# Pooled attention with a top-1 mixture of experts: other order of the first steps, pooling split anew, bias summed as a ninth head

## The chip, the cores and the metric

One NeuronCore of one Trainium2 chip runs the whole program. The metric is the device time of one execution in microseconds (us); the kernel before has a median of 625.47 us over 3 runs (623.34 to 629.04). Engines are named as in the profile: PE is TensorE (PEld its weight loads), DVE VectorE, ACT ScalarE, POOL GpSimd, and SP issues the DMAs. Each works through its own list of instructions in order.

## The reference, cut to what matters

```
q, k, v: (8 batches, 8 heads, 576 rows, 64)   x: 4608 tokens of 512   8 experts
k_p, v_p = mean of k, v over each 8 rows               # 72 pooled rows per head
attn     = softmax(q k_p^T / 8)                        # per head
x        = attn v_p, heads side by side                # one token per (batch, row)
logits   = x @ w_gate + modality_bias[modality_id]     # 8 per token
e        = argmax(logits);  g = softmax(logits)[e]
out      = g * (relu(x @ w1[e]) @ w2[e])
```

## The kernel before, in words

**Attention** runs in 20 steps. Two batches make five steps: (batch, 0), (batch, 1), a mixed one with the 64 last rows of both batches, then (next batch, 0), (next batch, 1). A step has two tiles of 128 tokens (the mixed one has one), so a group of two batches has 9 tiles. `steps[n]` names batch, half and tiles; the loop at the end of the attention part writes out, for each n, in which order every engine gets its instructions, and puts pieces of later batches in through the lists `hook_0`, `hook_1`, `hook_q`, `hook_2` and `hook_3`. That written order is the schedule: nothing reorders it but PE's early weight loads.

For one batch: `load_k`, `load_v`, `load_q` put DMAs on SP. `pool_k` and `pool_v` sum each 8 rows, either on POOL (`fold`, three additions of halves, L304 to L306) or on DVE (`reduce8`, L309). `k_operand` transposes the pooled keys on PE into `pk` (L340 for chunks 0 to 3 of 128 pooled rows, L343 for the rest) and ACT copies them twice into `kt` (L346, L347). The keys have two parts, chunks 0 to 2 and chunk 3 with the rest. `v_operand` copies the pooled values, multiplied by masks, into `vw` and `v4` (ACT L367, L368; for `v4` DVE or POOL L369) and transposes them (`pv`); `v_gate` multiplies them with the gate's weights (`pg`, L390, L391) into more columns of `vw` and `v4`, so that the product with the probabilities gives each head's share of the logits as well. For `v4` ACT copies the product (L396) and POOL multiplies it by the mask (L397).

For one step and one half w of the heads: `q_pe`, `q_act` transpose the queries (`pq`, L508) and copy them (`qt`, L514); `s_pe` makes the scores (`sc`, L533, mixed L527); `s_dve` takes maximum and difference (`mx` L540, `sb` L543); `s_act` the exponential (`pe`, L555, L556). For one tile: `t_pe`, `t_act` transpose and copy the probabilities (`pp` L562, `pt` L567), `t4_pe`, `t4_act` their last 64 columns (L574, L581); `a_pe` multiplies with the values (`av`, L597, L601); `x_dve` divides (`r`, `lg` L624, `xb` L630) and the rows are stored in DRAM.

**Routing**: when a group's tiles are through, `route` sums the heads' shares (`lgr`, L679), adds the bias (L680), finds maximum, softmax weight, expert and rank. These DVE instructions stand in a list from which `gap()` pops one or two between the instructions of a step. The bias per token, `bias_all`, comes from POOL (`modality_terms`, ending at L457).

**Experts**: 256 tokens to a slot, 18 slots at least (`NSTAT`). `part(s)` runs one slot: for each of 8 pieces f of the hidden width `first` (L170) and `second` (L1160) in three passes each. For the next slot POOL gathers rows (`gather`, L143), scales them (`scale`, L152), and PE transposes them (`x_transposes`, L161); `evac` empties the sums of the slot before, and POOL scatters them to the output (L1142), which `later` can put off until after `scale`.

## Time and profile before

| | |
|---|---|
| runs | 629.04, 623.34, 625.47 us; median 625.47 |
| profiled execution | 627.34 us, span 625.5 us from first to last instruction |
| granted TensorE clock, mean | 0.996 |
| PE busy | 601.5 us (96%) |
| DVE / ACT / POOL busy | 414.8 / 347.6 / 245.8 us |
| DMA | 76.58 MB, mean 122 GB/s |

A row of the timeline has start, time, engine, line, operation and tiles (out<-in), how many instructions it merges, and in brackets how long the engine had been idle and what ended that. A row of the windows has the stretch, its length, busy time and count of each engine in the order PE, PEld, DVE, ACT, POOL, then the granted clock, the DMA engines' busy share and GB/s.

### The profile page before, as it was taken

The page shows a single profiled execution, that of the slowest core. Times are in us where ns is not written, and L with a number is a line of the kernel's source. Part 1 is how long each engine was busy: PE and PEld are TensorE (multiplying, and loading weights), DVE is VectorE, ACT ScalarE, POOL GpSimd, SP SyncE. Part 2 cuts the span into 40 slices and gives each one's busy share as a digit, 9 for nine tenths or more (in the row PEclk, how much of TensorE's full clock was granted, in tenths as well). Part 3 has the DMA queues.
Part 4 walks back from the last instruction along what each step waited for, and adds up shares of the span by engine and source line. Part 5 has one row for each costly group of instructions (what it writes and reads, how often), then busy time and mean ns, then how long its engine had stood idle before and what let it go on. Part 6 is the DMA issues. An engine that isn't in the chain of part 4 may idle for free.

```text
span 625.5 us, 12457 instructions
## 1 busy us (share of the span) xinstructions
PE 601.5 (96%) x4223; PEld 545.5 (87%) x4223; DVE 414.8 (66%) x803; ACT 347.6 (56%) x657; POOL 245.8 (39%) x323
## 2 busy tenths in 40 slices
PE   4899999999999999999999999999999999999996
PEld 3689889888898998999999999999999899999995
DVE  4866798789957578675665665665665665666661
ACT  2667566788541455555555555555555555555551
POOL 5689978663000342422422413522522422422510
PEclk9999899999999999999999999999999999999999
DMA  8999969874202811201201452201205601201200
GB/s 244 287 313 311 357 186 369 279 232 124 86 36 70 271 70 33 69 29 43 70 28 42 130 190 89 67 33 37 70 34 172 202 23 36 69 30 40 70 35 21
DMA packets 63241, 76.58 MB, mean 122 GB/s; under 512 B 15423, under 2 KB 42047, under 8 KB 63168
## 3 DMA queue, kind: packets, MB, share of 16 engines
q1 hardware_dynamic: 57168, 55.98, 28.7%
q0 software_dynamic: 6000, 19.72, 9.7%
q8 instruction: 35, 0.57, 0.4%
q14 instruction: 38, 0.31, 0.2%
HBM read 119.40 MB, written 19.45 MB: 222 GB/s over the span
## 4 chain that ended last, share of the span: by engine, by line
PE 80%; DVE 7%; issue 4%; POOL 3%; DMA 3%; ACT 1%; SPq 0%; POOLq 0%; DVEq 0%; ACTq 0%
PE op L1160 31%; PE hp L170 30%; PE av L597 5%; PE sc L533 3%; PE xt L161 2%; PE av L601 2%; PE pq L508 2%; PE pp L562 2%; PE ph L170 1%; DMA out_dram<-ob,sidx 1%; DMA k<-in_k_dram 1%; DVE sb L543 1%; POOL v L304 1%; DVE mx L540 1%; DVE kp L309 1%
## 5 line engine op out<-in xcount | busy, mean ns | idle before, releaser
L136 ACT CAST hl<-raw 128x1024 fp32r<-128x1024 f32 x138 | 144.8, 1049 | 138.6 <-PE op L1160 137.6
L170 PE MATMUL hp<-xh,hl 128*128 128x256 f32 x1152 | 186.1, 284 | 0.0
L139 DVE TENSOR_TENSOR hl<-raw,hl 128x1024 fp32r<-128x1024 f32 x144 | 179.4, 1247 | 0.0
L170 PEld LDWEIGHTS hp<-xh,hl 128*128 128x128 f32 x1152 | 166.1, 189 | 10.5
L1160 PE MATMUL op<-hl,hh 128*128 128x512 f32 x554 | 173.5, 394 | 0.0
L174 DVE SCALAR_TENSOR_TENSOR hlo<-hp,hh 128x256 fp32r<-128x256 f32 x139 | 58.8, 423 | 132.3 <-ACT hh L172 132.3
L1142 POOL DMA_INDIRECT out_dram<-ob,sidx x36 | 50.4, 1400 | 226.4 <-DVE ob L1136 175.4
L1160 PE MATMUL op<-hl,hlo 128*128 128x512 f32 x277 | 108.4, 391 | 0.0
L1160 PEld LDWEIGHTS op<-hl,hh 128*128 128x128 f32 x554 | 94.8, 189 | 12.1
L170 PE MATMUL hp<-xl,hl 128*128 128x256 f32 x576 | 92.0, 282 | 0.0
L172 ACT ACTIVATE hh<-hp 128x256 fp32r<-128x256 f32 x139 | 53.4, 384 | 49.3 <-PE hp L170 48.9
L170 PEld LDWEIGHTS hp<-xl,hl 128*128 128x128 f32 x576 | 79.0, 190 | 0.0
L143 POOL DMA_INDIRECT xg<-xs,gidx x38 | 41.5, 1092 | 69.3 <-DMA raw<-in_moe_w_dram 53.8
L1160 PEld LDWEIGHTS op<-hl,hlo 128*128 128x128 f32 x277 | 52.0, 188 | 11.8
L152 POOL TENSOR_TENSOR xg<-xg 128x512 f32<-128x512 f32 x34 | 45.0, 1326 | 31.4 <-DMA xg<-xs,gidx 31.3
L597 PE MATMUL av<-vw,pt 128*128 128x146 f32 (+1 forms) x320 | 50.6, 297 | 1.9 <-ACT pt L567 1.1
L597 PEld LDWEIGHTS av<-vw,pt 128*128 128x128 f32 (+1 forms) x320 | 40.5, 183 | 4.1 <-ACT pt L567 2.2
L533 PE MATMUL sc<-kt,qt 128*128 128x144 f32 x256 | 38.5, 295 | 0.0
L533 PEld LDWEIGHTS sc<-kt,qt 128*128 128x128 f32 x256 | 34.8, 198 | 0.2
L540 DVE TENSOR_REDUCE mx<-sc 128x8 f32<-128x576 f32 (+1 forms) x40 | 27.7, 692 | 9.7 <-PE sc L533 8.1
L164 DVE TENSOR_TENSOR xl<-xt,xh 128x512 fp32r<-128x512 f32 x38 | 24.5, 684 | 14.4 <-ACT xh L163 14.4
L601 PE MATMUL av<-vw,pt 128*128 128x146 f32 (+1 forms) x160 | 31.3, 295 | 1.0 <-POOL vw L397 0.8
(234 smaller groups left out, 709.2 us busy)
## 6 DMA issues: line engine op xcount, KB each, us to landing
raw<-in_moe_w_dram SPq DMA_DIRECT2D x304, 256.0 KB
xs<-xb SPq DMA_DIRECT2D x16, 528.0 KB
k<-in_k_dram SPq DMA_DIRECT2D x7, 1024.0 KB
v<-in_v_dram SPq DMA_DIRECT2D x7, 1024.0 KB
q<-in_q_dram SPq DMA_DIRECT2D x6, 1024.0 KB
q<-in_q_dram SPq DMA_DIRECT2D x4, 512.0 KB
v<-in_v_dram SPq DMA_DIRECT2D x16, 128.0 KB
xs<-xb SPq DMA_DIRECT2D x8, 132.0 KB
```

What stands on the lines that cost most here:

```text
L136: nc.scalar.copy(hl[f][:, 0, :], raw[f])
L139: eng.tensor_sub(hl[f][:, 1, :], raw[f], hl[f][:, 0, :].bitcast(F32))
L143: nc.gpsimd.indirect_dma_start(out=xgs[(2 * s + tt) % len(xgs)], out_offset=None, in_=xs[0:rows, :], in_offset=IndirectOffsetOnAxis(idx[:, ...
L152: nc.gpsimd.tensor_tensor(xv, xv, x[:, RX:RX + H].rearrange("p (h o) -> p h o", o=1).to_broadcast([P, H, HD]), op=ALU.mult)
L170: nc.tensor.matmul(ph, hl[f][:, w, d * P:(d + 1) * P], x[:, d, :], start=(n == 0 and d == 0), stop=(n == 2 and d == ND - 1))
L172: nc.scalar.activation(hh, ph, AF.Relu)
L174: nc.vector.scalar_tensor_tensor(hlo, ph, 0.0, hh.bitcast(F32), op0=ALU.max, op1=ALU.subtract)
L533: nc.tensor.matmul(dst, qt[:, i, :], kt[b % NB][:, :, h * SPL:(h + 1) * SPL], start=True, stop=True)
L597: nc.tensor.matmul(av[hs, u, 2 * VC * gg:2 * VC * (gg + 1)], pt[:, c, hs], vw[y][:, c].rearrange("p a x -> p (a x)"), start=(gg == 0), sto ...
L601: nc.tensor.matmul(dst4[hs], pt4[:, hs], v4[y][:, 2 * u:2 * u + 2, :], start=False, stop=True)
L1142: nc.gpsimd.indirect_dma_start(out=out[:, :], out_offset=IndirectOffsetOnAxis(idx.bitcast(U32), 0), in_=ob, in_offset=None, bounds_check=N ...
L1160: nc.tensor.matmul(o[tt], l[:, ts_], hl[f][:, w, D:2 * D], start=(f == 0 and n == 0), stop=(f == NF - 1 and n == 2))
```

## The change

- **Start.** The queries of batch 0 are loaded by heads (4 heads, 1 KB runs) instead of by row pairs (512-byte runs), those of batch 1 in one transfer of 1 KB runs; the last value rows (`v4`) of batch 0 come ahead of the others. The first scores, `s_pe(0, 0)`, stand ahead of the keys' second part. `fill(n)` puts n products of a constant bf16 tile on PE, whose result nobody reads: 20, 5 and 5 after the three first key transposes, 6, 14 and 8 later.
- **Pooling.** Keys of batch 1: chunks 0 and 1 on POOL, 2 and 3 on DVE (before: 0 to 2 on DVE, 3 on POOL). Values of batches 1 and 2: chunk 3 on DVE. Values of batch 0: last rows first.
- **Order.** The keys of batch 1 become operands a little later (first part in `hook_q`, second in `hook_2` of step 1, behind chunk 3's reduction on DVE); the queries of step 3 are transposed in step 2; the values' masks (`v_operand`) stand ahead of the next keys' folds on POOL; `v_gate(0)` stands earlier.
- **Gate.** `v4`'s gate columns are multiplied on DVE straight from PSUM (L415); ACT's copy and POOL's product go.
- **Bias.** POOL copies it into a ninth place beside the 8 heads (`bias_in`), the sum runs over 9, the addition goes.
- **Division.** The reciprocal has a tile of its own; for some tiles ACT copies it beside the row.
- **Experts.** In slots 1 to 16 the scatters wait until after `scale`, so the gathers stand first.

```
-            if b < 2:
+            if b == 0:
                 for i in parts:
-                    nc.sync.dma_start(dst[:, :, 2 * HD * i:2 * HD * (i + 1)], src[:, :, 2 * HD * i:2 * HD * (i + 1)])
+                    nc.sync.dma_start(dst[:, 4 * i:4 * i + 4], src[:, 4 * i:4 * i + 4])
...
+        load_v4(0)
         load_v(0)
-        load_v4(0)
...
-                if b == 0 or (b == 1 and i == 0):
+                if b == 0:
...
-                        fold(t[:, c:m], kp[:, c:m])
+                        if b == 1 and c == 2:
+                            reduce8(t[:, c, :], kp[:, c, :])
+                        elif b > 1 or c < 2:
+                            fold(t[:, c:m], kp[:, c:m])
...
+        def fill(n):
+            t = ps_av.tile([P, 2, 512], F32, tag="av", name="fill")
+            for _ in range(n):
+                nc.tensor.matmul(t[:, 0, 0:P], iota_b, iota_b, start=True, stop=True)
...
+                if b == 0 and i == 0:
+                    fill(5 if j else 20)
...
+        def pool_k_rest(b):
+            reduce8(kraw[b][:, 3, :], kps[b][0][:, 3, :])
+        def pool_v_rest(b):
+            reduce8(vraw[b][:, 3, :], vps[b][0][:, 3, :])
...
+            nc.vector.tensor_tensor(d4[:, :, HD:HD + E], pg[:, 2, :].rearrange("p (j e) -> p j e", j=NPAIR),
+                                    m4b.to_broadcast([P, NPAIR, E]), op=ALU.mult)
...
-            nc.scalar.copy(vg4, pg[:, 2, :].rearrange("p (j e) -> p j e", j=NPAIR))
-            nc.gpsimd.tensor_tensor(d4[:, :, HD:HD + E], vg4, m4b.to_broadcast([P, NPAIR, E]), op=ALU.mult)
...
+        def bias_in(g):
+            t0, n = GROUPS[g]
+            nc.gpsimd.tensor_copy(lgs[g][:, :, H, :], bias_all[:, t0:t0 + n, :])
...
-            add(lambda: V.tensor_add(lg, lg, bias_all[:, sl, :]))
...
-                    at(hook_1, m, lambda b=b: k_operand(b + 1, 0))
-                    at(hook_1 if b == 0 else hook_q if b % 2 else hook_3, m, lambda b=b: k_operand(b + 1, 1))
+                    if b < 2:
+                        at(hook_2, m, lambda b=b: pool_v_rest(b + 1))
+                    at(hook_1 if b else hook_q, m, lambda b=b: k_operand(b + 1, 0))
+                    at(hook_2 if b == 0 else hook_q if b % 2 else hook_3, m, lambda b=b: k_operand(b + 1, 1))
...
+                    at(hook_1, m, lambda b=b: v_operand(b + 1))
                     if b + 2 < B:
-                        at(hook_0, m, lambda b=b: pool_k(b + 2))
-                    at(hook_1, m, lambda b=b: v_operand(b + 1))
+                        at(hook_1, m, lambda b=b: pool_k(b + 2))
...
+        fill(6)
+        s_pe(0, 0)
+        fill(14)
         pool_k(0, (1,))
+        s_dve(0, 0)
         token_ids()
...
-            if n == 1:
+            if n == 1 or n == 2:
                 q_pe(n + 1, 0)
                 q_act(n + 1, 0)
...
             if n == 0:
+                v_gate(0)
                 pool_k(1)
+            if n == 1:
+                pool_k_rest(1)
...
-                    if s == 1:
+                    if 0 < s < NSTAT - 1:
                         tail(later=later)
```

The change's effect on the lists of instructions is shown at three places. The first is DVE at the start: `mx_0`, `sb_0` are the first scores' maximum and difference, `vp` the pooled values of batch 0, `idt` to `w` constants. Before:

```order
L440 CAST idw<-idt 128x36
L441 TENSOR_SCALAR idt<-ids 128x36
L442 TENSOR_SCALAR idw<-idt 128x36
L444 TENSOR_SCALAR w_166<-iota_f 128x8
L540 TENSOR_REDUCE mx_0_260<-sc_0_255 128x8
L543 TENSOR_TENSOR sb_0_262<-sc_0_255,mx_0_260 128x576
L309 TENSOR_REDUCE vp_264<-v_127 128x64 x2
L540 TENSOR_REDUCE mx_1_303<-sc_1_298 128x8
```

With the change:

```order
L564 TENSOR_TENSOR sb_0_299<-sc_0_275,mx_0_297 128x576
L460 TENSOR_SCALAR idt<-ids 128x36
L461 CAST idw<-idt 128x36
L462 TENSOR_SCALAR idt<-ids 128x36
L463 TENSOR_SCALAR idw<-idt 128x36
L465 TENSOR_SCALAR w_166<-iota_f 128x8
L309 TENSOR_REDUCE vp_318<-v_130 128x64 x2
L561 TENSOR_REDUCE mx_1_359<-sc_1_354 128x8
```

The constants now stand behind the first scores; the second half's maximum still stands behind the pooled values.

The second place is PE in step 1, around the mixed step's first scores (`sc_0`, 64 rows): `pk` are keys of batch 1, `pq_0` the queries of step 3, `av` the product with the values for the second tile of step 0. Before:

```order
L527 MATMUL sc_0_448<-kt_133,qt_0_429 64x144
L527 MATMUL sc_0_448<-kt_134,qt_0_429 64x144
L508 MATMUL pq_0_454<-ident,q_215 128x128 x4
L597 MATMUL av_464<-vw_137,pt_427 128x146 x2
L601 MATMUL av_464<-vw_139,pt_1_136 128x2x73
```

With the change:

```order
L529 MATMUL pq_1_483<-ident,qm_195 128x128 x2
L349 MATMUL pk_0_486<-ident,kp_406 64x128 x3
L548 MATMUL sc_0_503<-kt_133,qt_0_477 64x144
L548 MATMUL sc_0_503<-kt_134,qt_0_477 64x144
L349 MATMUL pk_1_514<-ident,kp_406 64x128
L354 MATMUL pk_1_514<-ident,kp_1_407 64x64
L618 MATMUL av_519<-vw_137,pt_475 128x146 x2
```

Where the queries of step 3 stood is now the second part of batch 1's keys; on DVE its chunk 3 stands behind this step's maximum and difference:

```order
L561 TENSOR_REDUCE mx_0_508<-sc_0_503 128x2x2
L564 TENSOR_TENSOR sb_0_510<-sc_0_503,mx_0_508 128x2x144
L309 TENSOR_REDUCE kp_406<-k_191 128x64
L309 TENSOR_REDUCE vp_430<-v_210 128x64
L648 TENSOR_SCALAR r_526<-av_519 128x8
```

The third place is DVE where the first group's routing begins, in step 6. Before:

```order
L540 TENSOR_REDUCE mx_1_998<-sc_1_972 128x8
L679 TENSOR_REDUCE lgr_948<-lg_438 128x72
L680 TENSOR_TENSOR lgr_948<-lgr_948,bias_all 128x72
L543 TENSOR_TENSOR sb_1_1002<-sc_1_972,mx_1_998 128x576
L620 TENSOR_SCALAR r_1016<-av_991 128x8
```

With the change:

```order
L561 TENSOR_REDUCE mx_1_1066<-sc_1_1026 128x8
L708 TENSOR_REDUCE lgr_1002<-lg_492 128x72
L709 TENSOR_REDUCE m_0_1004<-lgr_1002 128x9
L564 TENSOR_TENSOR sb_1_1070<-sc_1_1026,mx_1_1066 128x576
L648 TENSOR_SCALAR r_1085<-av_1059 128x8
```

Between maximum and difference stand the sum and the tokens' maximum now, no longer the sum and the addition of the bias.

More of the change, by code (lines that the diff above doesn't have):

```diff
@@ L352, in pool_v @@
             t, t4 = vraw[b], v4raw[b]
+            if b == 0:
+                fold(t4, vp4)
             fold(t[:, 0:2], vp[:, 0:2])
-            if b:
+            if b > 2:
                 fold(t[:, 2:4], vp[:, 2:4])
+            elif b:
+                fold(t[:, 2], vp[:, 2])
             else:
@@ L358, in pool_v @@
                     reduce8(t[:, j, :], vp[:, j, :])
-            fold(t4, vp4)
+            if b:
+                fold(t4, vp4)
             vps[b] = (vp, vp4)
+        def pool_k_rest(b):
+            reduce8(kraw[b][:, 3, :], kps[b][0][:, 3, :])
+        def pool_v_rest(b):
+            reduce8(vraw[b][:, 3, :], vps[b][0][:, 3, :])
         m4b = m_4.rearrange("p (j o) -> p j o", o=1)
@@ L609, in x_dve @@
             if gi == 0:
-                lgs[g] = late_p.tile([P, GT, H, E], F32, tag="lg", bufs=2, name=f"lg_{g}")
+                lgs[g] = late_p.tile([P, GT, H + 1, E], F32, tag="lg", bufs=2, name=f"lg_{g}")
+                if g:
+                    bias_in(g)
             xw = xbs[n if n < NX0 else NX0 + n % (len(xbs) - NX0)]
@@ L617, in x_dve @@
             late = g >= EARLY_GROUPS and z == 1
-            r = xw[:, z, RX:RX + H].rearrange("p (u h) -> p u h", u=2) if late else s8
+            r = ap.tile([P, 2, 4], F32, tag="ri", bufs=4, name=f"ri_{t}")
             rb = r.rearrange("p u (h o) -> p u h o", o=1)
@@ L623, in x_dve @@
             gap(1)
-            nc.vector.tensor_tensor(lgs[g][:, gi].rearrange("p (u h) e -> p u h e", u=2), avv[:, :, :, HD:HD + E],
+            nc.vector.tensor_tensor(lgs[g][:, gi, 0:H].rearrange("p (u h) e -> p u h e", u=2), avv[:, :, :, HD:HD + E],
                                     rb.to_broadcast([P, 2, 4, E]), op=ALU.mult)
@@ L627, in x_dve @@
                 nc.scalar.copy(xo.rearrange("p (u h d) -> p u h d", u=2, h=4), avv[:, :, :, 0:HD])
+                nc.scalar.copy(xw[:, z, RX:RX + H].rearrange("p (u h) -> p u h", u=2), r)
             else:
@@ L850 @@
             at((hook_1, hook_2, hook_3)[(f + 1) % 3], N - 2 + (f + 1) // 3, lambda f=f: first0(f))
-        at(hook_0, 5, modality_terms)
+        at(hook_0, 5, modality_terms, lambda: bias_in(0))
         load_gate()
@@ L860 @@
         load_v4(1)
-        load_q(1, (0,))
-        load_q(1, (1,))
+        load_q(1)
         step_loads = {}
@@ L888 @@
         q_act(0, 1)
-        s_pe(0, 0)
-        s_dve(0, 0)
         pool_v(0)
         gate_operand()
+        fill(8)
         s_act(0, 0)
-        q_pe(1, 0)
-        q_act(1, 0)
         def run(hook, n):
@@ L936 @@
             if n == 0:
+                q_pe(1, 0)
+                q_act(1, 0)
                 v_operand(0)
@@ L957 @@
                 s_pe(n + 1, 0)
-            if nxt2 and n > 0:
+            if nxt2 and n > 1:
                 q_pe(n + 2, 0)
@@ L971 @@
                 x_dve(old[1])
-            if n == 0:
-                v_gate(0)
             gap(2)
@@ L982 @@
         last_route = route(len(GROUPS) - 1)
-        for fn in last_route[:7]:
+        for fn in last_route[:6]:
             fn()
@@ L1097 @@
     ]
-    lr, c4 = last_route, 2 * EARLY_SLOTS
+    lr, c4 = [None] + last_route, 2 * EARLY_SLOTS
     first_cols = table(c4, c4 + 6)
```

1 line of the change is left out of this document (removed).

## The prediction, on record before the changed kernel ran

> **What bounds the kernel now.** I read the page first, then the windows by stage, then the waits of PE, then the timeline where PE waits.
>
> ```profile
> span 625.5 us, 12457 instructions
> PE 601.5 (96%) x4223; PEld 545.5 (87%) x4223; DVE 414.8 (66%) x803; ACT 347.6 (56%) x657; POOL 245.8 (39%) x323
> ```
>
> ```profile
> 0.00:12.65 12.65, 3.69 (x12) 2.05 (x13) 6.58 (x14) 3.59 (x7) 6.95 (x43) 1.00 0.85 244
> 12.65:30.00 17.35, 14.28 (x95) 12.43 (x95) 12.68 (x20) 10.15 (x29) 11.04 (x20) 1.00 1.12 274
> 30.00:60.00 30.00, 28.11 (x238) 26.17 (x237) 18.32 (x48) 19.33 (x54) 26.40 (x46) 1.00 1.00 307
> 60.00:68.03 8.03, 8.03 (x68) 7.34 (x68) 5.72 (x13) 6.36 (x17) 7.38 (x14) 1.00 1.06 366
> 68.03:71.44 3.41, 2.05 (x17) 1.46 (x14) 3.41 (x10) 0.99 (x4) 3.17 (x5) 1.00 1.06 330
> 71.44:74.85 3.41, 3.41 (x15) 3.40 (x16) 2.73 (x12) 1.13 (x6) 3.02 (x8) 0.50 1.04 389
> 74.85:205.00 130.15, 127.13 (x1045) 115.44 (x1045) 105.58 (x337) 81.70 (x212) 54.32 (x87) 1.00 0.56 179
> 205.00:600.00 395.00, 395.00 (x2618) 359.34 (x2617) 251.11 (x341) 216.06 (x318) 129.80 (x102) 1.00 0.23 76
> ```
>
> PE is the bound. From 205 to 600 us it has no idle time at all, so nothing done there for POOL, DVE or the gathers can be seen, unless it makes PE wait. What can be won lies ahead: 9.0 us idle before 12.65, 3.1 to 30, 1.9 to 60, 1.4 in one stretch at 68 us, 3.0 from 75 to 205. The stretch at 68 costs twice: PE is busy for only 2.05 of 3.41 us, and in the next 3.41 us the granted clock is 0.50, so that another 1.7 us of PE's work is lost. Whatever moves PE's stream at 75 us moves the end by as much. So I follow PE from mark to mark.
>
> **The start.** PE waits for keys and queries, then DVE is behind:
>
> ```profile
> 8.59 1.12 PE L508 MATMUL pq<-ident,q 128*128 128x128 f32 x4 [0.56 <-DMA q<-in_q_dram]
> 9.74 0.59 ACT L514 COPY qt<-pq 128x512 f32<-128x512 f32 x1 [0.72 <-PE pq L508]
> 12.86 2.12 PE L533 MATMUL sc<-kt,qt 128*128 128x144 f32 x8
> 15.02 0.76 DVE L540 TENSOR_REDUCE mx<-sc 128x8 f32<-128x576 f32 x1 [2.55 <-PE sc L533]
> 16.49 2.01 DVE L309 TENSOR_REDUCE vp<-v 128x64 f32<-128x512 f32 x2
> 16.73 0.73 POOL L304 TENSOR_TENSOR v<-v 128x256 f32<-128x256 f32 x1 [0.84 <-DMA v<-in_v_dram]
> 18.41 0.76 DVE L540 TENSOR_REDUCE mx<-sc 128x8 f32<-128x576 f32 x1
> 21.31 0.66 PE L562 MATMUL pp<-ident,pe 128*128 128x128 f32 x4 [0.19 <-ACT qt L514]
> 27.07 0.60 PE L562 MATMUL pp<-ident,pe 128*128 128x128 f32 x4
> ```
>
> Four transposes take 1.12 us at 8.59 and 0.60 at 27.07, at the same clock in the profile's column: PE starts at half speed. The fills are to end that earlier, and they stand ahead of the keys. One bf16 product of 88 columns takes 58 ns by the row below, or 85 ns at 128 columns by proportion, and up to twice that at half speed; I take 0.11 us. Thirty of them, the three key transposes between (0.4 us each) and the first from 5.0 us put the query transposes at about 9.5 instead of 8.59. With 0.9 us for them and 0.6 for the copy, the first scores start at 11.0 instead of 12.86.
>
> ```profile
> L1050 PE MATMUL ptab<-bid,arow 128*128 128x88 bf16 x36 | 2.1, 207 | 0.0
> 11.00:13.00 2.00, 1.57 (x7) 1.18 (x7) 1.37 (x6) 0.62 (x2) 0.00 (x0) 1.00 1.05 381
> 24.50:28.50 4.00, 3.08 (x22) 2.62 (x23) 2.98 (x8) 2.36 (x6) 2.16 (x3) 1.00 1.15 267
> ```
>
> DVE then does maximum and difference (1.5 us) and the five constants (0.9), and is free for the pooled values at 14.6 to 15.6. Whether the values are there decides. Before, the last value rows came last and landed at 16.7 (POOL's row); now the big chunk comes last of the same bytes. But the queries go in 1 KB runs: 267 GB/s were moved while batch 1's 512-byte query runs went, 381 with the 2 KB runs of the values. So the start of the reductions lies between 14.6 and 16.7; I take 15.2, nearer to DVE than to the old landing, since 1 MB at 267 instead of some 330 GB/s costs 0.8 us. The second maximum behind them then stands at 17.2 instead of 18.5 and the first `pp`, 2.9 us behind it (18.41 to 21.31), at 20.0: **-1.3 us** (-1.9 to +0.2).
>
> From there to the mixed step's first scores:
>
> ```profile
> 21.21 0.73 POOL L304 TENSOR_TENSOR k<-k 128x256 f32<-128x256 f32 x1 [2.20 <-DMA k<-in_k_dram]
> 21.99 2.92 DVE L309 TENSOR_REDUCE kp<-k 128x64 f32<-128x512 f32 x3
> 22.48 0.63 ACT L555 ACTIVATE pe<-sb 128x512 f32<-128x512 f32 x1
> 25.30 0.47 ACT L346 COPY kt<-pk 64x384 f32<-64x384 f32 x1 [1.58 <-PE pk L340]
> 28.72 0.71 PE L527 MATMUL sc<-kt,qt 128*64 128x144 f32 x8
> 29.36 0.66 PE L508 MATMUL pq<-ident,q 128*128 128x128 f32 x4
> 29.48 0.46 DVE L540 TENSOR_REDUCE mx<-sc 128x4 f32<-128x288 f32 x1 [0.87 <-PE sc L527]
> 29.85 0.67 PE L597 MATMUL av<-vw,pt 128*128 128x146 f32 x4
> 30.04 0.46 DVE L543 TENSOR_TENSOR sb<-sc,mx 128x288 f32<-128x288 f32 x1
> ```
>
> Between the two `pp` (5.76 us) PE waited for three DVE reductions of batch 1's keys (2.92 us from 21.99). Now these transposes stand behind the second `pp`, and ACT sets the pace: it waits for DVE's new gate product (0.7 us after `pp`), then two gate copies, the copy of `pp`, an exponential and a tail copy (2.3), then the rest of `av` (1.2): 4.2, so the second `pp` at 24.2. Then transposes, two copies on ACT (1.0), keys (0.4), two copies of the keys (0.95), with the handovers 3.0: the mixed scores at 27.2 instead of 28.72, **-1.5** in sum.
>
> **The new wait.** Behind these scores PE now has `pk_1`, which needs chunk 3 of the keys, which DVE reduces after this step's maximum and difference. That is 0.56 from mx to sb, 0.5 for sb, 1.0 for a reduction (2.92/3) and handovers: PE stands still for 2.3 us; behind it in PE's list are `av`, the next `pp` and all that follows. Then 0.25 for the transposes: `av` starts at 27.2+0.7+2.3+0.25 = 30.45 instead of 29.85. And before, PE had used the time for step 3's queries (29.36 to 29.85), which it still owes: +0.5. PE stands at **+1.1**.
>
> This idle time, with 1 us ahead of it while the keys are copied, lies close to the case at 68 us: 1.36 us idle in 3.41 were followed by half a clock. I count one such window: +1.7, **+2.8** (bounds: none, or two, 0 to +3.4).
>
> The rule on this in the Trainium skill (TensorE: Matmul & The Clock Gate, Part 1) is that the clock falls to half after at least one idle window of about 3.4 us. By that rule 2.3 us would leave it alone, and the sum would be 1.7 us lower. The row at 68.03 speaks for a harsher one, since PE was busy there for 60% of the window.
>
> **POOL's waits.**
>
> ```profile
> PE pv L375 <- POOL vp L306: 1.1, 1, 1.1
> PE av L601 <- POOL vw L397: 0.8, 1, 0.8
> 34.61 1.27 POOL L304 TENSOR_TENSOR k<-k 128x512 f32<-128x512 f32 x1 [1.41 <-DMA k<-in_k_dram]
> ```
>
> Between 30 and 60 us PE waits twice for POOL, which is busy 26.4 of 30 us. The mask product now stands ahead of batch 2's folds and the gate product is gone, and DVE takes one chunk of the values of batches 1 and 2 (1.0 us of POOL's time each). POOL's folds of batch 2 cannot start before the keys land at 34.6, but PE, later by 2.8, needs them later too. Both waits go: -1.9, **+0.9**.
>
> **The stretch at 68 us.**
>
> ```profile
> 64.94 0.76 DVE L540 TENSOR_REDUCE mx<-sc 128x8 f32<-128x576 f32 x1 [0.53 <-PE sc L533]
> 65.61 1.20 DVE L679 TENSOR_REDUCE lgr<-lg 128x72 f32<-128x576 f32 x1
> 67.80 1.28 DVE L680 TENSOR_TENSOR lgr<-lgr,bias_all 128x72 f32<-128x72 f32 x1 [0.98 <-POOL bias_all L457]
> 69.00 0.74 DVE L543 TENSOR_TENSOR sb<-sc,mx 128x576 f32<-128x576 f32 x1
> 69.80 0.63 PE L390 MATMUL sc<-wgb,vt 128*128 128x32 f32 x4 [0.86 <-DVE sb L543]
> 71.26 1.20 PE L597 MATMUL av<-vw,pt 128*128 128x146 f32 x4 [0.50 <-DVE xb L630]
> ```
>
> DVE's addition of the bias waits 0.98 for POOL and takes 1.28; the difference `sb` stands behind it, and PE's gate product needs `sb`. Now DVE has the sum over nine (1.35) and a maximum (0.2) between mx and sb, and POOL is about 2 us earlier with the bias (a chunk of values, the mask and the gate product less after the keys' landing). So sb comes 1.6 us after mx has ended, not 3.3, 1.5 us ahead of PE's need. The 0.86 go, the window is then busy for 2.9 of 3.41, and the half clock behind it goes as well: 0.86+1.7 = -2.6. The 0.50 I leave: DVE's third routing step, which waits for ACT, now stands ahead of that `xb`. Sum: **-1.7**. If the half clock stays, 0; if the 0.50 go too, -3.1.
>
> The rest at nothing: the masks and the gate product (0.2 on DVE per batch) lie beside a busy PE, as do ACT's eight small copies; the scatters behind `scale` lie in the stage without PE idle time, and if the cover were gone, it would be `x_transposes` waiting for `scale`, which now comes earlier, not later. Filling stops before 15 us.
>
> **Sum.** -1.7 against the profiled execution's 627.34 us gives 625.6; its span is 625.5, the rest lies around it. That execution is 1.9 us above the median of the runs, so I forecast **623.8 us** for a median of 625.47.
>
> **Rivals.**
> - *No half clock after the new wait* (the skill's rule above): -3.4, 622.1 us. For it: the windows at 12.65 to 30 with 3.1 us idle show a clock of 1.00. Against it: the 68 us row. Chance 0.25.
> - *All goes well*: also values at DVE's pace (-0.6), the 0.50, and half of the 3.0 us idle after 75, where DVE has four additions less: about 619.8. Against it: those waits are routing in general. 0.12.
> - *Slower by the new wait*: the values land at 16.7 after all, so the first part is worth +0.2 instead of -1.3, PE idles from about 15.5 to 18.7 with its own half clock behind it (+1.7 more): +1.5, 627.0. It decides from a landing later than about 16 us. For it: the same bytes come first. 0.15.
> - *The change at 68 us does not do what it says*: POOL's bias copy stands behind all the folds as before, the sum now waits for it where earlier only the addition did, and the half clock stays: +0.9, 626.4. For it: POOL is busy 7.38 of 8.03 us there. 0.08.
>
> My forecast has 0.40. 1% (6.3 us) is about what a measurement of this kernel can tell from no change. Only the second rival comes near 619.2, so faster has 0.09; slower needs 631.7, beyond every case, and has 0.05 for what I have not seen; within 1% has 0.86. The range reaches over the rivals' times on both sides: 619.8 to 627.8; the forecast's own is 622.7 to 625.3 (the first part's bounds, and the 0.50).
>
> **What would show it.** In the profile after: first scores at 11 us; the pooled values of batch 0 on DVE from about 15; a PE wait of some 2.3 us for DVE ahead of the keys' second part at 28 to 30 us with a clock of 0.50 behind it; no PE wait for POOL from 30 to 60; at 68 us no wait for `sb` and a clock of 1.00; no idle PE from 205 to 600 us. A wait of 3 us or more at the keys, or an idle PE in the expert stage, would make me wrong.

## The result and the profile after

The changed kernel took 631.3 us in the median of its first five executions (630.5 to 636.03), the kernel before 625.47 beside it: ratio 1.0111, 95% interval 1.0062 to 1.0161. Five more gave 633.84 us, ratio 1.013 (1.0109 to 1.015). So it is 1.1 to 1.3% slower, where 623.8 us was forecast and 627.8 was the upper end of the range.

The page of the profiled execution, which took 633.02 us, and the same windows as shown of before:

```profile
span 631.3 us, 12554 instructions
PE 606.3 (96%) x4281; PEld 550.6 (87%) x4281; DVE 423.4 (67%) x808; ACT 348.2 (55%) x657; POOL 257.9 (41%) x319
```

```profile
12.65:30.00 17.35, 13.61 (x82) 12.02 (x80) 10.86 (x22) 8.99 (x24) 12.69 (x22) 0.80 1.10 309
30.00:60.00 30.00, 27.10 (x214) 24.57 (x215) 18.56 (x44) 18.23 (x50) 24.02 (x42) 0.94 1.01 306
60.00:68.03 8.03, 8.03 (x68) 7.75 (x68) 6.31 (x18) 5.19 (x14) 7.32 (x15) 1.00 1.06 360
68.03:71.44 3.41, 3.40 (x30) 3.16 (x28) 2.85 (x6) 3.21 (x10) 3.17 (x5) 1.00 1.05 348
71.44:74.85 3.41, 3.41 (x28) 2.90 (x29) 3.13 (x12) 2.27 (x6) 3.10 (x7) 1.00 1.06 392
74.85:205.00 130.15, 122.46 (x1012) 110.63 (x1011) 106.40 (x319) 80.89 (x214) 54.29 (x85) 1.00 0.53 167
205.00:600.00 395.00, 395.00 (x2619) 359.53 (x2618) 255.27 (x361) 214.54 (x316) 142.54 (x102) 1.00 0.24 78
```

The stretch at 68 us is full and its clock is 1.00. The clock is down in the first two windows instead, and PE has 122.46 us of work in 130.15 us behind 75 us, where it had 127.13. The expert stage has no idle PE in either kernel.

To say where the time went I use one mark per step: the start of the transposes of the last 64 columns (L574 before, L595 after, `sc<-ident,pe`), the first such row of each step in PE's timeline. Before, step 0 has it at 22.78 us, step 8 at 89.76, step 19 at 178.20; from there to the end of the span it is 447.3 us before and 447.0 after. The changes of a stretch's length, in us, beside the forecast of the prediction's steps (the first execution has half-clock windows at 19.02 to 25.84 and 32.67 to 36.08 us, the second at 30.02 to 36.84 and 101.69 to 105.11):

```
stretch            forecast   first profiled   second profiled
up to step 0         -1.3         +1.9             -0.7
steps 1, 2           +4.1         +4.1             +5.7    new wait, clock
steps 3, 4           -1.9         -1.8             -1.8    POOL's two waits
steps 5, 6           -2.6         -2.6             -2.6    the stretch at 68 us
steps 7, 8            0           +0.6             +0.6
steps 9, 10           0           +3.0             +4.7
steps 11 to 14        0           +1.4             +3.7
steps 15 to end       0           -0.8             -0.8
sum                  -1.7         +5.8             +8.8
```

Three of the rows that were costed came out to 0.1 us in the first execution. For steps 1 and 2 that is in part luck: the nine profiled executions with this wait (this kernel and versions of it, below) have one or two half-clock windows behind it, and 3.7 to 6.4 us in this row. What failed is the start, and what was put at nothing: steps 9 to 14.

**The start**, PE and then DVE in the timeline:

```profile
8.65 0.67 PE L529 MATMUL pq<-ident,q 128*128 128x128 f32 x4
10.08 1.22 PE L554 MATMUL sc<-kt,qt 128*128 128x144 f32 x8 [0.43 <-ACT qt L535]
17.13 0.33 PE L396 MATMUL pv<-ident,vp 128*128 128x128 f32 x1 [1.75 <-POOL vp L306]
```

```profile
16.03 1.98 DVE L309 TENSOR_REDUCE vp<-v 128x64 f32<-128x512 f32 x2 [1.49 <-DMA v<-in_v_dram]
```

PE reaches full speed earlier (these transposes take 0.67 us, not 1.12; in the run with the later keys below, with the same fillers, 1.06, and only the next four 0.66) and the first scores start at 10.08, 2.8 us earlier than before. But the values' reductions, forecast at 15.2, start at 16.03 (16.49 before), because DVE waits 1.49 us for the values' DMA; PE waits behind them, and in this execution the clock falls.

**The new wait** at the keys' second part, and at step 9 **a wait that the prediction did not have**:

```profile
30.03 0.70 PE L548 MATMUL sc<-kt,qt 128*64 128x144 f32 x6 [0.66 <-ACT kt L358]
32.86 0.39 PE L349 MATMUL pk<-ident,kp 128*64 128x128 f32 x1 [2.12 <-DVE kp L309]
98.99 0.60 PE L583 MATMUL pp<-ident,pe 128*128 128x128 f32 x4
102.23 1.25 PE L554 MATMUL sc<-kt,qt 128*128 128x144 f32 x8 [2.64 <-ACT vw L418]
```

The 2.12 us are the forecast's 2.3. The 2.64 us go from PE to ACT's gate copies, and these wait for DVE's gate product (L415). DVE in the same place, and POOL beside it:

```profile
101.71 0.29 ACT L417 ACTIVATE vw<-sc,m_a 128x32 f32<-128x32 f32 x1 [4.41 <-DVE vw L415]
```

```profile
94.81 1.49 DVE L765 TENSOR_SCALAR arow<-iota_b,rkf 128x128 bf16<-128x128 bf16 x1
97.62 1.28 DVE L775 TENSOR_TENSOR t<-e0oh,iota_f 128x8 f32<-128x8 f32 x1
99.20 0.73 DVE L561 TENSOR_REDUCE mx<-sc 128x8 f32<-128x576 f32 x1
100.27 0.65 DVE L779 TENSOR_SCALAR t<-rot 128x8 f32<-128x8 f32 x1
100.83 0.74 DVE L564 TENSOR_TENSOR sb<-sc,mx 128x576 f32<-128x576 f32 x1
101.50 0.18 DVE L415 TENSOR_TENSOR vw<-sc,m 128x32 f32<-128x32 f32 x1
```

```profile
94.98 1.27 POOL L304 TENSOR_TENSOR v<-v 128x512 f32<-128x512 f32 x1
97.61 1.27 POOL L304 TENSOR_TENSOR v<-v 128x512 f32<-128x512 f32 x1
100.17 0.72 POOL L304 TENSOR_TENSOR v<-v 128x256 f32<-128x256 f32 x1
```

DVE's L775 works on 8 columns, yet it takes 1.28 us and ends 0.02 us behind POOL's fold (98.90 and 98.88). L765 ends at 96.30 and the fold beside it at 96.25; L779 at 100.92, the fold at 100.89. `mx`, a reduction, and `sb`, which reads PSUM, take their usual 0.73 and 0.74 us beside the same folds. Some of DVE's short routing instructions sit out the whole fold. Before, this part of DVE's list had no fold beside it:

```profile
93.92 0.24 DVE L737 TENSOR_SCALAR arow<-iota_b,rkf 128x128 bf16<-128x128 bf16 x1
94.08 0.16 DVE L747 TENSOR_TENSOR t<-e0oh,iota_f 128x8 f32<-128x8 f32 x1
```

```profile
91.24 0.61 POOL L369 TENSOR_TENSOR vw<-vp,m 128x256 f32<-128x256 f32 x1
95.84 0.24 POOL L397 TENSOR_TENSOR vw<-vg,m 128x32 f32<-128x32 f32 x1 [3.99 <-ACT vg L396]
96.04 1.27 POOL L304 TENSOR_TENSOR v<-v 128x512 f32<-128x512 f32 x1
```

POOL stood still for 3.99 us ahead of its gate product, waiting for ACT's copy, and the value folds queued behind it until 96.04, when the routing was nearly through. The change took this product off POOL.

The Trainium skill (SBUF — State Buffer, Who interferes with whom) says that DVE and GpSimd share a pair of SBUF ports as an exclusive lock for a whole instruction, that a `tensor_scalar` in a two-port mode and an instruction with two SBUF inputs need it, and that a `tensor_reduce` on trn2 never does. The rows agree: 1.49 and 1.28 us for the two kinds, an unchanged 0.73 for the reduction. Whether L765 ran in such a mode the trace doesn't show.

### The profile page after: what moved, and what is told of

Same layout as the page of the kernel before. It is cut to its first block, busy times and chain, and to the rows that moved or that the text cites. A ratio compares the mean times of both kernels' runs of the same rounds, so it can differ in the third digit from the quotient of the medians.

```text
span 631.3 us, 12554 instructions
## 1 busy us (share of the span) xinstructions
PE 606.3 (96%) x4281; PEld 550.6 (87%) x4281; DVE 423.4 (67%) x808; ACT 348.2 (55%) x657; POOL 257.9 (41%) x319
## 4 chain that ended last, share of the span: by engine, by line
PE 66%; issue 4%; DMA 2%; DVE 1%; POOL 0%; POOLq 0%; ACT 0%; DVEq 0%
PE op L1193 30%; PE hp L170 30%; PE xt L161 2%; PE ph L170 1%; DMA out_dram<-ob,sidx 1%; PE av L618 1%; DMA xg<-xs,gidx 1%; PE ptab L1083 0%; DVE hl L139 0%; POOL xg L152 0%; PE av L622 0%; PE pp L583 0%; DVE mx L561 0%; DVE xl L164 0%; POOLq L1364 0%
## 5 line engine op out<-in xcount | busy, mean ns | idle before, releaser
L139 DVE TENSOR_TENSOR hl<-raw,hl 128x1024 fp32r<-128x1024 f32 x144 | 182.5, 1269 | 0.0
L143 POOL DMA_INDIRECT xg<-xs,gidx x38 | 55.7, 1464 | 219.8 <-DVE ob L1169 155.7
L152 POOL TENSOR_TENSOR xg<-xg 128x512 f32<-128x512 f32 x34 | 42.6, 1255 | 28.1 <-DMA xg<-xs,gidx 28.0
```

The source lines that it names most:

```text
L139: eng.tensor_sub(hl[f][:, 1, :], raw[f], hl[f][:, 0, :].bitcast(F32))
L143: nc.gpsimd.indirect_dma_start(out=xgs[(2 * s + tt) % len(xgs)], out_offset=None, in_=xs[0:rows, :], in_offset=IndirectOffsetOnAxis(idx[:, ...
L152: nc.gpsimd.tensor_tensor(xv, xv, x[:, RX:RX + H].rearrange("p (h o) -> p h o", o=1).to_broadcast([P, H, HD]), op=ALU.mult)
```

## The experiments

Each is shown as a difference to the changed kernel or to the one before. The kernel before had medians of 625.31 to 625.96 us beside them.

### The two suspected waits, PE's idle start, the bias alone

The gate copies ahead of the product:

```
-            nc.vector.tensor_tensor(d4[:, :, HD:HD + E], pg[:, 2, :]...
             nc.scalar.activation(dw[:, :, 0, HD:HD + E], pgv[:, :, 0, :], ...
             nc.scalar.activation(dw[:, :, 1, HD:HD + E], pgv[:, :, 1, :], ...
+            nc.vector.tensor_tensor(d4[:, :, HD:HD + E], pg[:, 2, :]...
```

> The changed kernel with one edit: ACT's two gate copies of a batch (L417, L418) stand ahead of DVE's gate product (L415) in the program instead of behind it; the product stays on DVE. Theory: the two ACT copies wait for DVE's product, which stands in DVE's list behind the routing of the previous group, and PE's scores wait for the copies (2.64 at 102.23 us, 0.65 at 118.43 us, 0.7 between 60 and 90 us). Then those waits of PE on vw L418 go, PE's marks at steps 8 to 11 lie 3 to 4 us earlier against the changed kernel, and the time is 3 to 4 us under it (about 627.5 to 628.5 us where the changed kernel has 631.3). Rival: DVE as a whole is late there, since it has the product and the sum over nine in a full list; then the wait only goes from the copies to PE's next need of DVE (the product's result or sb), the marks move by less than 1 us and the time stays within 1 us.

Measured 632.8 us, ratio 1.0115 (1.0085 to 1.0145): no gain. Step 9 is still 2.55 us longer (3.06 in the changed kernel). PE's waits from 88 to 112 us:

```profile
PE sc L554 <- DVE vw L417: 2.1, 1, 2.1
PE sc L595 <- DVE sb L564: 0.9, 1, 0.9
```

The theory falls: PE now waits for the product itself (L417 there), since the gate's result stands in the PSUM that the next scores need. DVE is late as a whole, as the rival had it.

The second part of the keys one hook later:

```
-  at(hook_2 if b == 0 else hook_q if b % 2 else hook_3, m, lambda b=b: k_operand(b + 1, 1))
+  at(hook_3 if b == 0 else hook_q if b % 2 else hook_3, m, lambda b=b: k_operand(b + 1, 1))
```

> The changed kernel with one edit: the transposes of the second part of batch 1's keys (pk_1) go from ahead of the first av to behind it, one hook later. Theory: PE's 2.1 us at pk_1 and the half-clock window behind it (1.7 us) come from the place of pk_1 ahead of work that was ready; moved behind av, the wait shrinks by the 1.2 to 1.7 us of PE's work that now stands ahead of it, the window is busy enough and the clock stays full: marks from step 2 on 3 to 4 us earlier against the changed kernel, the time about 627.5 to 628. Rival A: the wait goes and the half clock stays (it comes from the idle time as a whole around it): 2 us. Rival B: the wait moves along with the transposes, since av itself or the next pp waits for DVE: 0 to 1 us.

Measured 628.58 us, ratio 1.0049 (1.0029 to 1.0068), 2.7 and 5.3 us under the changed kernel's two medians. Step 1 is 0.43 us longer than before, not 3.06, PE's wait there shrinks to this row, and there is no half-clock window behind it:

```profile
PE pk L349 <- DVE kp L309: 0.5, 1, 0.5
```

So this wait, its size and its clock were read rightly. The kept profiles agree: nine executions have a wait of 2.1 us here, and each has half clock behind it; five have the later keys and a wait of 0.5 us, and none has it.

Thirty more fillers (`fill(30)`) ahead of `v_operand(0)`:

> The changed kernel with one addition: 30 more of the small products without use (88 columns, bf16) on PE ahead of batch 0's values, where PE stood idle from 15.4 to 17.1 us. Theory: the two half-clock windows from 19.02 to 25.84 us are set by PE's idle time in the windows before them; kept busy, PE has full clock there, and step 0's mark lies 1.9 us or more earlier (24.69 to about 22.5), the time some 2 us under the changed kernel's. Rival: PE isn't the bound there but DVE with its reductions and differences; then the clock is full and the marks of steps 0 and 1 move by less than 0.5 us. A second rival: the half clock has another cause than idle time and stays.

Measured 632.81 us, ratio 1.0123 (1.0095 to 1.0152). Step 0's mark lies at 21.92 us. The run with the gate copies first, which has no filler there and no half clock either, has it at 22.13: the first rival holds, and at full clock PE isn't the bound there. As the half clock is missing from both, this run doesn't tell why the clock falls at 19 us in some executions; the profiles together do ("The start and the gathers", below). In the trace the fillers have 128 columns, not 88.

The bias alone, in the kernel before (`bias_in`, nine summands, no addition):

> The kernel before with the bias alone changed: copied by POOL as a ninth head, summed with the heads, no addition on DVE. Theory (the prediction's step at 68 us): the wait for sb at 69.80 and the half-clock window from 71.44 go, 2.6 us: marks unchanged to step 5, 2.6 us earlier from step 6 on, the time 2.6 us under the kernel before (about 622.9 where it has 625.5). Rival: the wait at 68 us only went because the changed kernel comes there 4 us later with other work on POOL; then the sum waits for POOL's bias as the addition did, and the time stays within 1 us.

Measured 626.1 us, ratio 1.0012 (0.9992 to 1.0032). Steps 5 and 6 grew by 0.93 us instead of shrinking by 2.6: DVE's sum now waits for POOL's copy where the addition had waited for POOL's bias, and PE waits 0.81 us for `sb`, where it had waited 0.86.

```profile
66.69 1.34 DVE L686 TENSOR_REDUCE lgr<-lg 128x72 f32<-128x648 f32 x1 [2.40 <-POOL lg L606]
68.20 0.75 DVE L543 TENSOR_TENSOR sb<-sc,mx 128x576 f32<-128x576 f32 x1
```

### Which part lets the folds meet the routing

The folds ahead of the mask again, from batch 1 on:

```
+                    if b == 0:
+                        at(hook_1, m, lambda b=b: v_operand(b + 1))
-                    at(hook_1, m, lambda b=b: v_operand(b + 1))
                     if b + 2 < B:
-                        at(hook_1, m, lambda b=b: pool_k(b + 2))
+                        at(hook_0 if b else hook_1, m, lambda b=b: pool_k(b + 2))
+                    if b:
+                        at(hook_1, m, lambda b=b: v_operand(b + 1))
```

> The changed kernel with one part undone: from batch 1 on, the next keys' folds stand ahead of the values' mask on POOL again, as before; for batch 0's step the new order stays. Theory: the mask (L391) waits for PE to have read the old values of the tile that it writes (4.71 us at 86.97, 7.31 at 109.13, 5.61 at 129.69 in the changed kernel's trace) and holds the folds behind it in POOL's list; they then run beside DVE's routing, where DVE's short instructions last as long as POOL's fold beside them (1.49 and 1.28 us, 0.2 and 0.16 before), sb and the gate product come late, and PE waits 2.64 us. Undone, POOL's folds start at about 83 us, DVE's rows are short again, step 9's mark lies about 3 us earlier against the changed kernel and those from 11 on 3.5 to 4.5: the time about 3.5 to 4 us under the changed kernel's. Rival A: DVE is late because of the sum over nine and the gate product, whatever POOL does; then less than 1 us. Rival B: the early mask is what took the stretch at 68 us away; then that wait comes back (2.5 us) and the gain is 1 us or so.

Measured 633.87 us, ratio 1.0142 (1.0119 to 1.0165). Step 9 is still 2.71 us longer: the mask's place isn't the cause there. Steps 5 and 6 are 1.5 us shorter than before, so of the 2.6 us at 68 us only 1.1 came back, where rival B had 2.5.

The gate columns of `v4` on ACT and POOL again:

```
-            nc.vector.tensor_tensor(d4[:, :, HD:HD + E], pg[:, 2, :]...
...
+            vg4 = ap.tile([P, NPAIR, E], F32, tag="vg4", bufs=1, name=f"vg4_{b}")
+            nc.scalar.copy(vg4, pg[:, 2, :]...
+            nc.gpsimd.tensor_tensor(d4[:, :, HD:HD + E], vg4, ...
```

> The changed kernel with one part undone: v4's gate columns are copied by ACT and multiplied by POOL again, no gate product on DVE. Theory (the folds stall DVE): sb on DVE is just as late, PE waits for it instead of for the copies, and step 9's mark moves by less than 1 us; time within 1 us of the changed kernel's. Rival (the product on DVE is the cause): the 2.64 us and the 0.65 go, step 9 to 11 lie 3 us or more earlier, time 3 to 4 us less.

Measured 628.7 us, ratio 1.0045 (1.0021 to 1.007). The rival holds on the time: steps 9 to 11 are 0.1 us longer than before, not 3.8. And POOL and DVE show why:

```profile
96.66 0.24 POOL L419 TENSOR_TENSOR vw<-vg,m 128x32 f32<-128x32 f32 x1 [2.95 <-ACT vg L418]
96.86 1.27 POOL L304 TENSOR_TENSOR v<-v 128x512 f32<-128x512 f32 x1
```

```profile
94.72 0.24 DVE L766 TENSOR_SCALAR arow<-iota_b,rkf 128x128 bf16<-128x128 bf16 x1
94.88 0.16 DVE L776 TENSOR_TENSOR t<-e0oh,iota_f 128x8 f32<-128x8 f32 x1
```

POOL is held by the gate result again, its fold starts at 96.86, and the routing instructions ahead of that are short. My theory had the collision right and its origin wrong: I had looked for it in the mask.

The early mask alone, in the kernel before (from batch 1 on):

> The kernel before with one part done alone: from batch 1 on the values' mask stands ahead of the next keys' folds on POOL. Theory: the same stall appears without the rest of the change: POOL waits for PE at the mask, the folds run beside DVE's routing, DVE's short instructions there grow to 1 us and more, and steps 8 to 9 take 2 to 3 us longer than before; the time 2 to 4 us over the kernel before. Rival: it needs the gate product or the nine summands on DVE too; then steps 8 to 9 take as long as before and the time stays within 1 us (or falls by some tenths where POOL's waits go).

Measured 625.8 us, ratio 1.0011 (0.9991 to 1.0032). Step 9 is unchanged: the theory falls a second time. But steps 5 and 6 shrink by 2.3 us, most of the 2.6 at 68 us. The bias addition there:

```profile
67.05 0.63 DVE L680 TENSOR_TENSOR lgr<-lgr,bias_all 128x72 f32<-128x72 f32 x1 [1.08 <-POOL bias_all L457]
```

```profile
66.98 0.61 POOL L369 TENSOR_TENSOR vw<-vp,m 128x256 f32<-128x256 f32 x1
```

The 1.28 us of this addition before were the fold beside it, in the kernel before:

```profile
67.72 1.27 POOL L304 TENSOR_TENSOR k<-k 128x512 f32<-128x512 f32 x1
```

Beside the shorter mask the addition takes 0.63. The gain is paid back at steps 12 to 14, 3.4 us in this execution, 1.7 of it a half-clock window at 129.45 us. It is the stall that the theory expected, one group later. POOL waits 5.15 us for PE at the mask, its fold of keys comes late, and DVE's next routing, an instruction of 9 columns that took 0.13 us in the kernel before, meets it; PE then waits 2.33 us for `sb`, where it had waited 0.49:

```profile
122.32 1.27 POOL L304 TENSOR_TENSOR k<-k 128x512 f32<-128x512 f32 x1
122.42 1.20 DVE L732 TENSOR_SCALAR rkm<-rki 128x9 int32<-128x9 int32 x1
128.09 0.30 PE L574 MATMUL sc<-ident,pe 128*128 128x128 f32 x1 [2.33 <-DVE sb L543]
```

Later keys and folds ahead of the mask together:

> The changed kernel with two edits: the second part of batch 1's keys one hook later (which by itself gave 628.58 us against 625.49 of the kernel before) and the folds ahead of the mask from batch 1 on. Theory: the two causes stand at different places and add up: the marks from step 9 on lie 1 to 3 us ahead of the kernel before, no half-clock window of the new wait, time 624 to 625 us, 1 us under the kernel before or more. Rival: the folds ahead of the mask make POOL late for the bias or the values again as before, 626 to 627 us.

Measured 630.2 us, ratio 1.0081 (1.0055 to 1.0107): 1.6 us worse than the later keys alone. Step 9 is 3.11 us longer, the collision stays. The theory's second half was wrong, since the gate product was still on DVE.

### The collision and its origin, shown directly

POOL without the value folds of batches 3 to 7:

```
-            fold(t[:, 0:2], vp[:, 0:2])
-            if b > 2:
-                fold(t[:, 2:4], vp[:, 2:4])
+            if b < 3:
+                fold(t[:, 0:2], vp[:, 0:2])
+            if b > 2:
+                nc.gpsimd.memset(vp, 0.0)
```

> The changed kernel without POOL's folds of the values of batches 3 to 7 (their pooled values are set to zero, only the folds of the last rows stay), to see what the folds cost DVE beside them; the gate product stays on DVE. Theory (collision): DVE's short routing rows last 1.49, 1.28, 0.64 us because POOL's folds of the values run beside them, so that sb and the gate product come 2.5 to 3 us late. Without the folds these rows take 0.2 and 0.16 us again, PE's wait for the gate copies is under 0.5 us, and step 9's mark lies 2.5 to 3 us earlier against step 8's than in the changed kernel (7.4 to 8 us between the two marks less the start, as 8.37 in the kernel before). Rival (place in the list): the product is late because it stands behind routing and sb in DVE's list; then the wait of 2 us or more stays without the folds.

Step 9 is 0.71 us longer than before instead of 3.06, PE's wait for the gate copies is 0.4 us, and DVE's rows are short wherever no fold is left:

```profile
95.78 0.24 DVE L766 TENSOR_SCALAR arow<-iota_b,rkf 128x128 bf16<-128x128 bf16 x1
95.94 0.16 DVE L776 TENSOR_TENSOR t<-e0oh,iota_f 128x8 f32<-128x8 f32 x1
```

```profile
PE sc L555 <- ACT vw L419: 0.4, 1, 0.4
```

So 2.35 of the 3.06 us are the folds beside DVE, and at most 0.7 the product's place in DVE's list; one routing row still takes 1.19 us at 93.72, beside the last rows' fold that was left. The time as a whole, 634.74 us (ratio 1.0144, 1.0111 to 1.0177), says nothing here: the zeros change the result, and the span behind the last mark is 452.5 us instead of 447.0. That the routing then picks other experts is likely, and not shown.

The gate product on DVE alone, in the kernel before:

```
+            nc.vector.tensor_tensor(d4[:, :, HD:HD + E], pg[:, 2, :]...
             nc.scalar.activation(dw[:, :, 0, HD:HD + E], pgv[:, :, 0, :], ...
...
-            vg4 = ap.tile([P, NPAIR, E], F32, tag="vg4", bufs=1, name=f"vg4_{b}")
-            nc.scalar.copy(vg4, pg[:, 2, :]...
-            nc.gpsimd.tensor_tensor(d4[:, :, HD:HD + E], vg4, ...
```

> The kernel before with one part done alone: the gate product on DVE straight from PSUM, ahead of ACT's two gate copies; no copy on ACT and no product on POOL for it. Theory: POOL's next folds of the values no longer wait for the gate result (3.99 us at 95.84 in the kernel before), start about 4 us earlier, run beside DVE's routing, and steps 8 to 9 take 2 to 3 us longer than the 8.37 us of before; similar once more at step 13. Time 2 to 5 us over the kernel before. Rival: with the mask behind the folds POOL is late enough, no collision; time within 1 us.

Measured 631.32 us, ratio 1.0087 (1.0059 to 1.0115). Steps 9, 11 and 14 are 3.1, 2.5 and 3.1 us longer, two half-clock windows (94.82 and 139.19 us) among it; step 1 is 2.7 us longer, with a half-clock window at 26.55 us. This one part, done alone, makes the kernel 0.9% slower, most of the 1.1 to 1.3% of the whole change:

```profile
89.35 0.61 POOL L369 TENSOR_TENSOR vw<-vp,m 128x256 f32<-128x256 f32 x1
89.92 1.26 POOL L304 TENSOR_TENSOR v<-v 128x512 f32<-128x512 f32 x1
92.47 1.27 POOL L304 TENSOR_TENSOR v<-v 128x512 f32<-128x512 f32 x1
```

```profile
89.11 2.29 DVE L736 TENSOR_SCALAR arow<-iota_b,rkf 128x128 bf16<-128x128 bf16 x2
92.60 1.19 DVE L736 TENSOR_SCALAR arow<-iota_b,rkf 128x128 bf16<-128x128 bf16 x1
```

POOL goes from the mask straight into the fold at 89.92, where before it had stood still from 91.85 to 95.84, and DVE's rows grow as in the changed kernel.

At 68 us the same move helps, which the theory didn't have: steps 5 and 6 are 2.85 us shorter, with the bias still added by DVE. POOL has the bias at 64.07 us instead of 67.76, and the addition waits neither for it nor for a fold that was there first, and takes 0.23 us:

```profile
66.58 0.23 DVE L679 TENSOR_TENSOR lgr<-lgr,bias_all 128x72 f32<-128x72 f32 x1
```

### The versions that follow from it

Later keys and the gate columns on ACT and POOL:

> The changed kernel with the second part of batch 1's keys one hook later, and the gate columns on ACT and POOL as before. By itself the first gave 628.58 and the second 628.7 us, where the changed kernel has 631 to 632 and the kernel before 625.4. Theory: they act at different places (steps 0 to 1, steps 8 to 11), so both gains add: marks 3 to 4 us ahead of the kernel before at step 9, then 1 to 3 lost at steps 12 to 14 as in the single runs; time 624 to 625.5. Rival: each moves POOL against DVE, the collision comes back at another step, and the time is 627 or more.

Measured 624.52 us, ratio 0.9983 (0.9965 to 1.0001). The two gains add: step 9's mark lies 4.55 us ahead of the kernel before, and 1.5 are lost again up to step 19. The interval reaches to 1, so this is no clear gain over the kernel before.

The same, with the mask behind the folds from batch 2 on:

> As the run with the later keys and the gate columns on ACT and POOL, and with the values' mask behind the folds again from batch 2 on (for the steps of batches 0 and 1, where it took POOL's waits and the stretch at 68 us away, the new order stays). Theory: what the early mask lost at steps 12 to 14 (3 us, half of it a half-clock window) goes too; marks 3 to 4 us ahead of the kernel before from step 6 to the end, time about 622, faster than both kernels. Rival: the folds then wait elsewhere, no difference from the run without this edit.

Measured 624.79 us, ratio 0.9972 (0.9951 to 0.9993). The marks lie 2.5 us ahead of before from step 7 to the end, in an execution with two half-clock windows at 17.89 to 24.72 us; steps 12 to 14 lose nothing. That is 0.3% under the kernel before, but not the 622 forecast.

### The start and the gathers

The start's order undone and no fillers, on the changed kernel and on the last version (the same edit):

```
-            for _ in range(n):
+            for _ in range(0):
...
-        fill(6)
-        s_pe(0, 0)
-        fill(14)
         pool_k(0, (1,))
-        s_dve(0, 0)
...
+        s_pe(0, 0)
+        s_dve(0, 0)
         pool_v(0)
         gate_operand()
-        fill(8)
```

> The changed kernel with the order at the start undone: the first scores stand behind the keys' second part again, and no fillers; the loads stay as changed. If the reordered start is worth what the undisturbed executions showed (0.7 us), step 0's mark lies at about 22.8 us without a half-clock window, as in the kernel before, and the time is 0.7 us over the changed kernel's. Rival: the fillers and the early scores only make PE idle later, between 15.4 and 18 us, and bring the half-clock windows from 19 us; then the start undone has no such window there and the time is 1 to 2 us under the changed kernel's.

> The same on the best version so far (later keys, gate columns on ACT and POOL, mask behind the folds from batch 2 on; 624.79 us where the kernel before had 625.96, ratio 0.9972): the start undone as well. 0.7 us slower if the start is worth that, 1 to 2 us faster if it brings the half-clock windows.

Measured 632.65 us, ratio 1.0107 (1.0083 to 1.0131), and 623.64 us, ratio 0.9966 (0.9945 to 0.9987). Neither differs from its base by what these intervals resolve. All profiled executions together say more: where DVE starts on the values, and step 0's mark, in us from the span's start:

```
scores' order as before (6 executions):  scores 11.99 to 13.13, values 15.62 to 16.77, mean 16.22; mark 6.3 us behind the values
order as changed (12 executions):        scores  9.77 to 10.74, values 15.04 to 17.05, mean 15.75; mark 6.2 to 6.3 us behind them in eight,
                                         7.5 to 8.8 in the four with half clock from 18 to 19 us on
```

At full clock the mark hangs on the values, not on the first scores. These come 2.3 us earlier, the values 0.5 by the means, and they spread by 1 to 2 us between executions of either order, so that even the 0.5 is uncertain.

The half clock from 18 to 19 us shows in four of the twelve and in none of the six with the old order. Within an execution all half-clock stretches start whole multiples of 3.41 us apart (19.02 and 32.67 us in the changed kernel's first: 4 times 3.41), so the clock goes by a fixed grid of windows of that length. Here is the window in which PE waits for the values, in the changed kernel's first execution (half clock follows) and in the run with the gate copies first (none follows):

```profile
15.60:19.02 3.42, 1.28 (x9) 1.09 (x10) 2.95 (x4) 1.38 (x4) 1.82 (x6) 1.00 1.13 291
```

```profile
16.03:19.44 3.41, 1.87 (x14) 1.68 (x15) 3.38 (x5) 1.66 (x6) 1.20 (x5) 1.00 1.18 262
```

PE is busy there for 0.92 to 1.73 us in the four executions, and in the other eight for 1.87 us or more in each window from 13 to 21 us. So it depends on when the values land and on where the windows lie: the early scores leave PE idle for longer ahead of the values, and the half clock comes when enough of that falls into one window.

The gathers' order undone:

```
-                    if 0 < s < NSTAT - 1:
+                    if s == 1:
                         tail(later=later)
```

> The changed kernel with the gathers' order undone: in slots 2 to 16 the scatters stand ahead of scale again. PE has no idle time from 205 to 600 us in either kernel, so the time stays within 0.5 us of the changed kernel's. Rival: the scatters and gathers use DMA queues and POOL so that one order makes PE wait in the expert stage; then PE shows idle time there, and the span beyond the last mark of the first stage (447.0 us in the changed kernel, 447.3 before) differs by more than 1 us.

Measured 633.34 us, ratio 1.0136 (1.0105 to 1.0168); the changed kernel beside it 633.84. The rival shows in the trace: PE waits twice in the expert stage for POOL to scale the gathered rows, and the span behind the last mark is 449.8 us instead of 447.0.

```profile
PE xt L161 <- POOL xg L152: 2.3, 2, 1.2
```

Before, the same order makes no PE wait; why it does here stays open, and the times don't resolve it.

The changed kernel once more:

> The changed kernel once more, for more executions beside the kernel before: ratio 1.010 to 1.013, mean time lost to half-clock windows 4 to 5 us against 2 to 2.6. In its profile the waits at the keys' second part (2.1 us), for the gate copies at 102 us (2.6 us) and no wait at 68 us come again; the half-clock windows from 19 us need not.

Measured 633.84 us, ratio 1.013 (1.0109 to 1.015). The three waits came as expected, without the windows from 19 us, but with one at 101.69 us behind the wait for the gate copies. From span and mean clock of each execution, the time lost to half clock is estimated at 5.5 us in the mean of the changed kernel's ten executions and 2.2 in the 84 of the kernel before that ran beside the experiments. So of the 7.4 us between their means (633.3 and 625.9), some 3 are clock and the rest is waiting.

## Why the prediction was wrong

- **The start**, forecast -1.3 us: +1.9 and -0.7. PE did its part better than forecast (first scores at 10.08 instead of 11.0), but the step "whether the values are there decides" took 15.2 where 15.75 was the mean of twelve: by the means the reorder is worth 0.5 us, not 1.3, and a spread of 2 us lies over it. The first execution has the third rival's place and mechanism as well (idle from 15.4 to 17.1, half clock behind).
- **The new wait**: 2.12 us, forecast 2.3, with one window of half clock in the first execution and two in the second. The mechanism was right, and that one window was counted is luck: four of the nine executions with this wait have one, five have two. Taking it away by the later keys brought 2.7 us or more. The rival without half clock fell.
- **POOL's two waits**: -1.85, forecast -1.9. Right.
- **The stretch at 68 us**: -2.56, forecast -2.6, by a reason that was in part wrong. That POOL comes earlier with the bias was right: the gate product's move alone brings 2.85 us there by it. The early mask alone brings 2.3 in another way, by putting the short mask and not the fold beside the addition. Both leave the addition in. The change of the bias itself brings nothing: alone it made the stretch longer by 0.9 us, by the last rival's mechanism. And the 1.28 us that I read as the price of the addition were POOL's fold beside it (0.23 in the run with the gate product alone); the row at 67.80 and POOL's fold could have told. That `sb` would come 1.5 us ahead of PE's need was a slip as well: by the rows shown (ready at 68.04, needed at 68.94) it was 0.9.
- **The rest at nothing**: this is the step that failed. "The masks and the gate product (0.2 on DVE per batch) lie beside a busy PE" counted the 0.18 us of the product and not what leaving POOL does. POOL's wait of 3.99 us for the gate copy looked free. It kept POOL's folds off DVE's routing. Without it steps 9 and 10 lose 3.0 us in one execution and 4.7 in the other, and with the product back on ACT and POOL they lose nothing. Steps 11 to 14 lose 1.4 and 3.7 us. There the masks have a part: with the product back 1.3 us of loss stay (with the later keys too), and go when the masks stand behind the folds again as well (-0.2). The product alone on the kernel before gives 631.32 us; the change without it, 628.7, and with the later keys as well, 624.52.

None of the signs that the prediction had named for its being wrong showed: the wait at the keys was 2.12 us, not 3, and PE isn't idle in the expert stage. One of its sums was off without bearing on this: the second rival's terms, put on top of the first rival's, add up to 619.5 us, not 619.8.

What stays open: why one half-clock window follows the new wait in some executions and two in others, the 0.6 us at steps 7 and 8, and the idle PE in the expert stage when the gathers' order is undone.

## What to carry to other kernels

An instruction taken off an idle-looking engine also takes away the wait that held that engine's later work back: follow what starts earlier, and what it then runs beside. When a DVE instruction of 8 columns takes over a microsecond, look at POOL's row with the same end before taking the duration as its price. Where two engines block each other, an order is best judged by the marks of each step in the trace, since gains and losses of 3 us cancelled here within one kernel.

## What the runs showed of the hardware

- Some of DVE's short instructions wait for POOL's to end: L775 took 1.28 us beside a fold of 1.27, and 0.16 without. In the run with the gate product alone, one took 2.13 us and waited through two of POOL's instructions that followed each other without a gap (89.35 to 91.18; the merged row of 2.29 us at 89.11). Reductions and the instructions that read PSUM showed no such wait: in eight of the profiles, `sb` with 576 columns took at most 0.76 us, 148 times beside an instruction of POOL and 107 times alone, and so did `mx` over as many (154 and 101).
- The half clock came behind 2.12 us of PE's idle time at 32.86 us, and one or two windows of it, by execution. The Trainium skill (TensorE: Matmul & The Clock Gate, Part 1) speaks of a window of about 3.4 us that is idle; here less was enough. In all 18 profiles from 13 to 215 us, each of the 16 full-clock windows with PE busy for 1.6 us or less was followed by half clock, 7 of the 23 with 1.6 to 2.1 us were, and none with more.
